# Head of a gated spectral block on one core: the adaptive scale moved into a DFT table, grad_out gated and turned inside the first loop, and the third frequency chunk packed

## The chip, the cores and the metric

The kernel runs on one core of a Trainium2 chip. The metric is device time in microseconds, as the median of repeated executions. The profile is one execution, read as busy times, waits and a chain of releases on the core's engines: PE (TensorE, matrix multiplications), DVE (VectorE), ACT (ScalarE), POOL (GpSimd) and SP (SyncE, here only an issuer of DMAs).

## The reference, cut to what matters

The reference is the forward pass and all gradients of one transformer-like block with 2048 tokens (S) of width 576 (D). With `sa, ca, ga, sb, cb, gb` made from a condition vector `c`:

```python
mod = (silu(c) @ w_mod).reshape(1, 6, 1, 576)      # sa, ca, ga, sb, cb, gb
h = layernorm(x) * (1 + ca) + sa
x = x + ga * irfft2(rfft2(h) * (w_r + 1j * w_i))   # over tokens and width
h = layernorm(x) * (1 + cb) + sb
x = x + gb * (((h @ w_gate) * (h @ w_up)) @ w_down)   # width 4608 inside
# returned: x, and the gradients of x, w_r, w_i, w_gate, w_up, w_down, c, w_mod
```

The gradients need, early on, `grad_out * gb` in two layouts: with tokens on partitions (called `gon` in the kernel) and with width on partitions (`goT`).

## The kernel before, in words

Everything is bf16 with fp32 sums in PSUM. The 2048 tokens are 16 tiles of 128; the width of 576 is four chunks of 128 and one of 64. A Fourier transform is a series of matrix multiplications with tables: `RD` (cosine and sine over the width), `G1` and `BD2` (two steps over the tokens), and `BDA`, `GB`, `IR` for the way back. The 289 frequencies are padded to `FP` = 292, which is 73 groups of 4, taken in 19 chunks (`NCH`) of up to 16 frequencies.

The framework orders instructions itself: each engine has a queue in a fixed order, found at compile time by a list scheduler that follows the program order as priority and simulates durations. `tc.issue_after(x)` puts the instructions of its block behind `x` on `x`'s own queue. At run time an engine works through its queue in order and waits where an input or a buffer isn't ready.

The stages, with the stretches of the profiled execution:

- **Head, 0 to 70 us.** `mod_load`/`mod_make` (L236, L242) multiply the condition by a slice of `w_mod` and leave a row, the same on all partitions, in `modh`. Then `pipeline` runs `s1_norm`, `s1_cols`, `s1_rows` (L284 to L331) over the 16 tiles. `s1_norm` makes the layer norm on ACT (`n1`, L297), multiplies by `1+ca` (L299) and adds `sa` (L301) on DVE, and turns the tile with five PE transposes (L306). `s1_cols` multiplies by `RD` (ten matmuls, L315) and `s1_rows` by `G1` (four, L329 and L330); the result is kept in `VA`. After that loop in program order, `grad_out` is turned tile by tile with six transposes (L347), and two DVE multiplications by a column form of `gb` (`gbT`, read back from `modb_d`) leave `goT` (L348, L349).
- **Chunks, 70 to 134 us.** `s2_turn`, `s2_filter`, `s2_back`, `s2_inv` run over the 19 frequency chunks: transposes, `BD2`, multiplication by the filter, transposes, `BDA`; the planes `A_h` are kept. `u4_groups` put in between them multiply `w_down` by `goT` (L377) and keep the result in DRAM.
- **Way back, 134 to 217 us.** `s3_rows` (six matmuls per tile, L470 and L471), `s3_cols` (twelve, L485) and `s3_norm`, with two `u4_groups` per tile. `s3_norm` loads `x` again in pairs of tiles (`xc`, L495), adds, and makes the second layer norm.
- **Rest of `u4_groups`, 217 to 282 us,** and beside it, on DVE, the multiplication of `gon` by `gb` (L519).
- **Main loop, 282 to about 1280 us,** over 36 blocks of 128 of the inner width: the gated products and their gradients.
- **Tail, about 1280 to 1593 us.** `t1_*`, `t2_*` and `t3_*` are the backward counterparts of the three transform stages; `t3_rows` and `t3_cols` (L1009, L1010, L1022) have the same six and twelve matmuls per tile. The last product with `w_down` (L1113, `u3p`) is put by the scheduler beside them and goes on alone afterwards.

In `s3_rows` and `t3_rows` the 292 frequencies are covered by three windows of 128 that start at `FS = [0, 128, 164]`; the third overlaps the second, and `IR` is zero in the overlap:

```python
for fc in range(3):
    f0 = FS[fc]
    o = upa[:, fc, :] if fc < 2 else upb[:, 0, :]
```

For each window two matmuls of 256 columns follow, one for each plane.

Of the kernel before, what the change touches and what calls it, by code (L numbers as in the profile page):

```python
# [26 lines left out]
EPS = 1e-5  # L27
KD = [128, 128, 128, 128, 64]
RM = [slice(0, 128)] * 4 + [slice(64, 128)]
FS = [0, 128, FP - 128]  # L30
# [5 lines left out]
def _tables():  # L36
# [4 lines left out]
    for m in range(5):  # L41
        d = 128 * m + q
        valid = d < D
# [19 lines left out]
    IR = np.zeros((128, 3, 2, D), f8)  # L63
    d = np.arange(D)
    for fc in range(3):
        ff = FS[fc] + q
        valid = (ff < DF) & (ff >= 128 * fc)
        cf = np.where((ff == 0) | (ff == DF - 1), 1.0, 2.0) / (D * S) * valid
        ang = 2 * np.pi * np.outer(ff, d) / D
        IR[:, fc, 0, :] = np.cos(ang) * cf[:, None]  # L70
        IR[:, fc, 1, :] = -np.sin(ang) * cf[:, None]
# [7 lines left out]

TABS = dict(RD=[128, 5, 2, FP], G1=[128, NT, 3, 128], GB=[128, NT, 3, 128], BD2=[128, 128], BDA=[128, 128], IR=[128, 3, 2, D])  # L80


def build(ctx, tc, A_x, A_w_r, A_w_i, B_w_gate, B_w_up, B_w_down, c_in, w_mod, grad_out,
# [72 lines left out]

    def pipeline(n, steps):
# [26 lines left out]
    gonf = res2.tile([128, NT * D + 64], BF, name="gon")  # L184
    gon = gonf[:, 0:NT * D].rearrange("p (t d) -> p t d", t=NT)

    with ExitStack() as hs:
# [17 lines left out]
        modh = [(u4 if j == MGB else hp1).tile([128, D], BF, name="modh%d" % j) for j in range(6)]  # L205
        VA = hp1.tile([128, NG * 128], BF, name="VA")
        hpp = hp1.tile([128, 3, DP], BF, name="hpp")
        nc.gpsimd.memset(hpp[:, :, D:DP], 0.0)
        nc.gpsimd.memset(gonf[:, NT * D:NT * D + 64], 0.0)
# [13 lines left out]
        nc.vector.tensor_tensor(out=sc_col[:], in0=c_f[:], in1=sig[:], op=MUL)  # L223
        tmp5 = hp1.tile([128, 5], FP32, name="tmp5")
# [4 lines left out]
        sc_bf = hp1.tile([128, 5], BF, name="sc_bf")  # L229
        nc.vector.tensor_copy(sc_bf[:], sc_col[:])  # L230
        nc.vector.tensor_copy(sc_col[:], sc_bf[:])
# [10 lines left out]
        def mod_make(j, wm, eng="v"):  # L242
# [8 lines left out]
            return nc.sync.dma_start(modb_d[:, j, :], modh[j][:]).ins  # L251
# [13 lines left out]
        x_load(0)  # L265
        wms[MSA] = mod_load(MSA)
        T = {"RD": load_table(hp1, "RD", "tA")}
        T["G1"] = load_table(hp1, "G1", "tB")
        mod_make(MCA, wms[MCA])
        first = mod_make(MSA, wms[MSA], "a")  # L270
        with tc.issue_after(first):
            x_load(1)
            wms[MGB] = mod_load(MGB)
            nc.sync.dma_start(gon, go_v)
            x_load(2)
            T["BD2"] = load_table(hp1, "BD2")
            T["BDA"] = load_table(hp1, "BDA")

# [3 lines left out]
        gbT = hp1.tile([128, 5], BF, name="gbT")  # L282

        def s1_norm(t):  # L284
# [6 lines left out]
            if t == 0 or tt == (1 if c4 == 0 else 0):  # L291
                n = 1 if t == 0 else 4 - tt
                nmr = norm_stats(xts[c4][:, tt:tt + n, :], hw2, n, "ln1", rstd1g[:, t:t + n], 4)
                for k in range(n):
                    n1s["nmr", t + k] = nmr[:, k:k + 1]
            n1 = n1s[c4]
            nc.scalar.activation(out=n1[:, tt, :], in_=xts[c4][:, tt, :], func=ACT.Identity, bias=n1s["nmr", t], scale=rstd1g[:, t:t + 1])  # L297
            nm = hw2.tile([128, D], BF, name="nm")
            nc.vector.tensor_tensor(out=nm[:], in0=n1[:, tt, :], in1=modh[MCA][:], op=MUL)  # L299
            hh = hpp[:, t % 3, :]  # L300
            nc.vector.tensor_tensor(out=hh[:, 0:D], in0=nm[:], in1=modh[MSA][:], op=ADD)  # L301
            if tt == 3:
                nc.gpsimd.dma_start(n1_d[:, t - 3:t + 1, :], n1[:])
            pt = fps.tile([128, 5, 128], BF, name="trp", tag="fp")
            for m in range(5):
                nc.tensor.transpose(pt[:, m, :], hh[:, m * 128:(m + 1) * 128], ident[:])  # L306
            hT = hTs[t] = hw2.tile([128, 5, 128], BF, name="hT")
            evac(hT[:], pt[:], eng="a")

        def s1_cols(t):  # L310
            zt = zts[t] = hw2.tile([128, 2, FP], BF, name="zt", bufs=3)
            for cc in range(2):
                zp = fps.tile([128, 512], FP32, name="zp", tag="fp")
                for m in range(5):
                    mm = nc.tensor.matmul(zp[:, :FP], lhsT=hTs[t][:, m, :], rhs=T["RD"][:, m, cc, :], start=(m == 0), stop=(m == 4))  # L315
                evac(zt[:, cc, :], zp[:, :FP], eng="a")
            if t == 1:
                with tc.issue_after(mm.ins):
                    mod_make(MGB, wms[MGB], "a")
                with nc.allow_non_contiguous_dma(reason="tiny column load"):  # L320
                    nc.sync.dma_start(gbT[:, 0:4], modb_d[0, MGB, 0:512].rearrange("(m q) -> q m", q=128))
                    for r in (0, 64):
                        nc.sync.dma_start(gbT[r:r + 64, 4:5], modb_d[0, MGB, 512:576].rearrange("(m q) -> q m", q=64))
# [9 lines left out]
        pipeline(NT, [s1_norm, s1_cols, s1_rows])  # L333
# [8 lines left out]
        goT = u4.tile([128, NT, 5, 128], BF, name="goT")  # L342
        for t in range(NT):
            pt = u4ps.tile([128, 6, 128], BF, name="u4p")
            for m in range(6):
                c0 = t * D + m * 128 if m < 5 else t * D + 448
                nc.tensor.transpose(pt[:, m, :], gonf[:, c0:c0 + 128], ident[:])  # L347
            nc.vector.tensor_tensor(out=goT[:, t, :, :], in0=pt[:, 0:5, :], in1=gbT[:].unsqueeze(2).to_broadcast([128, 5, 128]), op=MUL)  # L348
            nc.vector.tensor_tensor(out=goT[64:128, t, 4, :], in0=pt[64:128, 5, :], in1=gbT[64:128, 4:5].to_broadcast([64, 128]), op=MUL)  # L349
# [39 lines left out]
        A_h = pool("hA", 1).tile([128, 2, NT, FP], BF, name="A_h")  # L389
        with ExitStack() as rc:  # L390
# [16 lines left out]
            def s2_filter(ci):  # L407
                g0, ng, f0, w = dims(ci)
                xp = fps.tile([128, 4, 128], FP32, name="xp", tag="fp")
                for j in range(ng):  # L410
                    nc.tensor.matmul(xp[:, j, :], lhsT=VTs[ci][:, j, :], rhs=T["BD2"][:], start=True, stop=True)
# [21 lines left out]
            def s2_inv(ci):  # L433
# [4 lines left out]
                Ac = A_h[:].rearrange("k c a f -> k (c a) f")[:, :, f0:f0 + w].rearrange("k e (j f) -> k j e f", f=4)  # L438
                evac(Ac, ap_[:, 0:ng, :].rearrange("k j (e f) -> k j e f", f=4), eng="a")
# [23 lines left out]
        def s3_rows(sa):  # L463
            ut = uts[sa] = hw2.tile([128, 3, 256], BF, name="ut", bufs=3)
            upa = fps.tile([128, 2, 256], FP32, name="upa", tag="fp")
            upb = fps.tile([128, 2, 256], FP32, name="upb", tag="fp")
            for fc in range(3):
                f0 = FS[fc]
                o = upa[:, fc, :] if fc < 2 else upb[:, 0, :]
                nc.tensor.matmul(o, lhsT=A_h[:, 0, sa, f0:f0 + 128], rhs=T["GB"][:, sa, 1:3, :].rearrange("k v s -> k (v s)"), start=True, stop=False)  # L470
                nc.tensor.matmul(o, lhsT=A_h[:, 1, sa, f0:f0 + 128], rhs=T["GB"][:, sa, 0:2, :].rearrange("k v s -> k (v s)"), start=False, stop=True)  # L471
            evac(ut[:, 0:2, :], upa[:], eng="a")
            evac(ut[:, 2, :], upb[:, 0, :], eng="v")

        def s3_cols(sa):
# [4 lines left out]
            for h in range(2):  # L480
                yp = fps.tile([128, 512], FP32, name="yp", tag="fp")
                k = 0
                for fc in range(3):
                    for cc in range(2):
                        nc.tensor.matmul(yp[:, 0:288], lhsT=ut[:, fc, cc * 128:(cc + 1) * 128], rhs=T["IR"][:, fc, cc, h * 288:(h + 1) * 288], start=(k == 0), stop=(k == 5))  # L485
                        k += 1
# [222 lines left out]
    with ExitStack() as ts:  # L709
# [108 lines left out]
        with ExitStack() as r1:  # L818
# [44 lines left out]
            def t1_turn(t):  # L863
                pt = ps_fp.tile([128, 5, 128], BF, name="trp", tag="fp")
                for m in range(5):
                    nc.tensor.transpose(pt[:, m, :], rings["gyr"][:, t % 3, wide(m)], ident[:])
# [53 lines left out]
        A_ = pool("rb", 1, "right", stack=rB).tile([128, 2, NT, FP], BF, name="j_A")  # L920
# [20 lines left out]
        with ExitStack() as r2:  # L941
# [35 lines left out]
            def t2_inv(ci):  # L977
# [4 lines left out]
                nc.scalar.copy(A_[:].rearrange("k c a f -> k (c a) f")[:, :, f0:f0 + w].rearrange("k e (j f) -> k j e f", f=4), ap_[:, 0:ng, :].rearrange("k j (e f) -> k j e f", f=4))  # L982
# [19 lines left out]
        def t3_rows(sa):  # L1002
            ut = uts[sa] = c3.tile([128, 3, 256], BF, name="ut", bufs=3)
            upa = ps_fp.tile([128, 2, 256], FP32, name="upa", tag="fp")
            upb = ps_fp.tile([128, 2, 256], FP32, name="upb", tag="fp")
            for fc in range(3):
                f0 = FS[fc]
                o = upa[:, fc, :] if fc < 2 else upb[:, 0, :]
                nc.tensor.matmul(o, lhsT=A_[:, 0, sa, f0:f0 + 128], rhs=T["GB"][:, sa, 1:3, :].rearrange("k v s -> k (v s)"), start=True, stop=False)  # L1009
# [203 lines left out]
```

## Time and profile before

| | us |
|---|---|
| median of 3 runs | 1591.95 (1589.98 to 1597.13) |
| the profiled execution's own time | 1594.8 |
| its span, first to last instruction | 1593.0 |
| PE busy | 1535.0 (96%) |
| DVE busy | 1045.6 (66%) |
| ACT busy | 559.8 (35%) |
| PE busy in 0 to 70 us | 53.4 of 70 |
| PE busy in 70 to 134 us | 64.0 of 64 |
| PE busy in 134 to 217 us | 75.7 of 83 |
| PE busy in 282 to 1280 us | 995.4 of 998 |
| PE busy in 1412 to 1462 us (`t3`) | 47.8 of 50 |
| PE busy in 1462 to 1577 us | 114.6 of 115 |

A matmul's busy time in the profile contains its way through the array, and matmuls overlap; what one costs a full PE is the distance from its start to the start of the next. The mean granted PE clock is 0.992 of full speed.

### The profile page before, as it was taken

The numbers are of one execution on the slowest core, as the hardware profiler recorded it, in microseconds if no ns is written. First come the engines' busy times: TensorE is split into PE (matmuls) and PEld (weight loads), VectorE is DVE, ScalarE is ACT, GpSimd is POOL, SyncE is SP. The second block draws the span as 40 slices with busy tenths as digits, with TensorE's granted clock in tenths as the row PEclk, the third lists the DMA queues.
The fourth block names the chain that finished last, engine by engine and source line by source line (L and its number), as shares of the span: only waits on it lengthen the run. The fifth ranks groups of instructions, "written<-read, shape, count | busy, mean of one in ns | idle before, by whom it ended". The sixth has DMA issues, their size and how long they took to land.

```text
span 1593.0 us, 30039 instructions
## 1 busy us (share of the span) xinstructions
PE 1535.0 (96%) x11370; PEld 1035.0 (65%) x11370; DVE 1045.6 (66%) x2626; ACT 559.8 (35%) x1108; POOL 170.3 (11%) x283
## 2 busy tenths in 40 slices
PE   6999989999999999999999999999999989899997
PEld 4666533567666666766666676666666666677775
DVE  6866763666666666666666666666666774678655
ACT  6666632322222222222222222222222365466022
POOL 0001212101010100101010010101000011100232
PEclk9999999999999999999999999999999999999998
DMA  9869998779877686786868686767857786635775
GB/s 319 275 194 237 242 259 228 166 139 143 141 152 150 130 177 104 158 152 134 162 130 144 140 171 118 164 133 129 180 103 143 191 264 197 218 112 179 286 224 159
DMA packets 485252, 280.64 MB, mean 176 GB/s; under 512 B 407633, under 2 KB 452434, under 8 KB 484210
## 3 DMA queue, kind: packets, MB, share of 16 engines
q1 hardware_dynamic: 459922, 185.65, 55.1%
q0 software_dynamic: 25184, 93.07, 19.8%
q8 instruction: 89, 1.46, 0.4%
q14 instruction: 57, 0.47, 0.1%
HBM read 108.77 MB, written 82.31 MB: 120 GB/s over the span
## 4 chain that ended last, share of the span: by engine, by line
PE 77%; DMA 9%; DVE 7%; issue 3%; ACT 2%; SPq 0%; POOL 0%; DVEq 0%; ACTq 0%; POOLq 0%
PE u57p L572 26%; PE u8p L654 17%; PE gup L625 16%; PE u4p L377 7%; PE gup L620 2%; DMA xc<-in_A_x_dram 2%; DMA n2c<-n_d 2%; DMA Xn<-xn_d 2%; DMA wmj<-in_w_mod_dram 1%; DMA wdB<-in_B_w_down_dram 1%; DVE pr L803 1%; PE u3p L1113 1%; PE yp L485 1%; PE yp L1022 1%; PE zp L315 1%
## 5 line engine op out<-in xcount | busy, mean ns | idle before, releaser
L659 DVE TENSOR_TENSOR acc<-acc,u8p 128x288 f32<-128x288 f32 x1088 | 489.2, 454 | 314.6 <-PE u8p L654 314.2
L654 PE MATMUL u8p<-wT,ggT 128*128 128x288 bf16 x1152 | 327.5, 286 | 2.1 <-DVE acc L659 2.1
L654 PE MATMUL u8p<-wT,guT 128*128 128x288 bf16 x1152 | 327.2, 286 | 0.0
L625 PE MATMUL gup<-h2T,wgu 128*128 128x512 bf16 x1152 | 294.9, 379 | 0.0
L575 ACT CAST so<-u57p 128x288 bf16<-128x288 f32 x216 | 86.0, 398 | 521.4 <-PE u57p L572 515.6
L572 PE MATMUL u57p<-gon,hh_sf 128*128 128x288 bf16 x1152 | 188.6, 286 | 0.4 <-DMA hh_sf<-hhT 0.4
L572 PE MATMUL u57p<-h2p,gg_sf 128*128 128x288 bf16 x1152 | 187.6, 286 | 0.0
L572 PE MATMUL u57p<-h2p,gu_sf 128*128 128x288 bf16 x1152 | 186.2, 286 | 0.0
L625 PEld LDWEIGHTS <-wgu 128*128 128x128 bf16 x1152 | 109.5, 98 | 98.8 <-issue 17.1
L654 PEld LDWEIGHTS <-ggT 128*128 128x128 bf16 x1152 | 112.6, 98 | 67.2 <-issue 14.0
L377 PE MATMUL u4p<-goT,wdT 128*128 128x512 bf16 x656 | 151.1, 379 | 4.4 <-DVE ghh_st L141 3.8
L654 PEld LDWEIGHTS <-guT 128*128 128x128 bf16 x1152 | 112.7, 98 | 56.2 <-issue 2.6
L1113 PEld LDWEIGHTS <-hl 128*128 128x128 bf16 x1152 | 111.5, 98 | 35.7 <-issue 7.5
L572 PEld LDWEIGHTS <-hh_sf 128*128 128x128 bf16 x1152 | 112.6, 98 | 29.0 <-DMA hh_sf<-hhT 0.7
L572 PEld LDWEIGHTS <-gu_sf 128*128 128x128 bf16 x1152 | 112.5, 98 | 28.4
L572 PEld LDWEIGHTS <-gg_sf 128*128 128x128 bf16 x1152 | 112.5, 98 | 28.3
L627 ACT CAST gT<-gup 128x512 bf16<-128x512 f32 x144 | 84.3, 585 | 130.4 <-PE gup L625 130.4
L377 PEld LDWEIGHTS <-wdT 128*128 128x128 bf16 x656 | 61.9, 98 | 77.2 <-issue 11.5
L627 ACT CAST uT<-gup 128x512 bf16<-128x512 f32 x144 | 84.3, 585 | 73.6 <-PE gup L625 73.6
L1113 PE MATMUL u3p<-wdB,hl 128*128 128x288 bf16 x672 | 94.8, 288 | 8.0 <-DMA wdB<-in_B_w_down_dram 7.0
L638 POOL DMA_DIRECT2D hhT_d<-hhT x36 | 33.2, 921 | 504.4 <-DVE hhT L629 475.4
L139 ACT CAST ghh_st<-u4p 128x512 bf16<-128x512 f32 x88 | 51.1, 585 | 68.1 <-PE u4p L377 67.7
(358 smaller groups left out, 1734.0 us busy)
## 6 DMA issues: line engine op xcount, KB each, us to landing
ghhT_d<-ghh_st POOLq DMA_DIRECT2D x36, 512.0 KB, 4.7
ghh<-ghhT_d POOLq DMA_DIRECT2D x36, 512.0 KB, 7.3
hhT_d<-hhT POOLq DMA_DIRECT2D x36, 512.0 KB, 6.6
hl<-hhT_d SPq DMA_DIRECT2D x32, 576.0 KB, 6.9
out_dram<-woT SPq DMA_DIRECT2D x72, 128.0 KB, 2.0
wdn<-in_B_w_down_dram SPq DMA_DIRECT2D x18, 288.0 KB, 4.3
out_dram<-so SPq DMA_DIRECT2D x36, 144.0 KB, 2.6
wgu<-in_B_w_gate_dram SPq DMA_DIRECT2D x18, 256.0 KB, 3.4
```

Of the source, the lines that this page charges most:

```text
L139: nc.scalar.copy(dst, src)
L315: mm = nc.tensor.matmul(zp[:, :FP], lhsT=hTs[t][:, m, :], rhs=T["RD"][:, m, cc, :], start=(m == 0), stop=(m == 4))
L377: nc.tensor.matmul(pt[:], lhsT=wdTs[k][:, j, m, :], rhs=goT[:, 4 * sb4:4 * sb4 + 4, m, :], start=(m == 0 and n == 5), stop=(m == n - 1))
L572: mm = nc.tensor.matmul(pw[0][:, 0:288], lhsT=sf[:, t, :], rhs=rhs_n[:, t, h * 288:(h + 1) * 288], start=(t == 0), stop=(t == NT - 1))
L575: nc.scalar.copy(so[:, h * 288:(h + 1) * 288], pw[0][:, 0:288])
L620: nc.tensor.matmul(pts[-1][:], lhsT=wgu[r, 8, jw * 128:(jw + 1) * 128], rhs=h2T[r, 4 * sb4:4 * sb4 + 4, 4, :], start=True, stop=False)
L625: nc.tensor.matmul(pts[k][:], lhsT=wgu[:, 4 * wi_ + m, jw * 128:(jw + 1) * 128], rhs=h2T[:, ts_, m, :], start=False, stop=(m == 3))
L627: nc.scalar.copy((gT, uT)[wi_][:, ts_, :], pts[k][:])
L638: nc.gpsimd.dma_start(hhT_d[:, :, fb, :].rearrange("tp f x -> f tp x"), hhT[:].rearrange("f (tp ti) p -> f tp (ti p)", ti=2))
L654: nc.tensor.matmul(pu[:, 0:288], lhsT=l_, rhs=r_, start=(k == 0), stop=(k == len(mms) - 1))
L659: nc.vector.tensor_tensor(out=dst, in0=dst, in1=pu[:, 0:288], op=ADD)
L1113: mm = nc.tensor.matmul(p2[:, 0:288], lhsT=hls[fb // 9][:, fb % 9, ti * 128:(ti + 1) * 128], rhs=(wdA[:, fb] if fb < 15 else wdB[:, fb - 1 ...
```

## The change

1. **The scale goes into the table.** `mod_cols` makes `1+ca` as a column (25 matmuls with one column of output); five DVE operations multiply the chunks of `RD` by it, giving `RDm`, and `s1_cols` uses `RDm`. Only the plain layer norm `n1` is turned. Chunks of the width now start at `M0 = [0, 128, 256, 384, 448]`, and the table is zero where the last overlaps, so the zero-padded buffer `hpp` is gone.
2. **The shift goes to frequency zero.** A row added to all tokens only changes the zero token frequency. `shift_rows` computes S times the transform of `sa` once (ten matmuls and a few DVE operations, kept in `zr` as a high and a low part), and each `s2_filter` adds it with one small matmul (`first_k`).
3. **`n1` is made on DVE** with one operation instead of on ACT, and its statistics (`s1_stats`) are made two tiles ahead, in pairs.
4. **`gon` is gated first and turned afterwards**, inside the loop (`go_turn`): one DVE multiplication per tile, five transposes, one plain copy (three of four on ACT). `gon` has 640 columns per tile, and the last 64 are loaded again to fill it. The column `gbT`, its three loads, and the later DVE multiplication of `gon` are gone.
5. **The loop is written out** with lags: norm 0, stats 2 ahead, turn 1, cols 2, rows 4, `go_turn` 6.
6. **Loads.** The `RD` table is loaded ahead of the second slice of `w_mod`; the next loads are queued behind the load of `G1` and no longer behind the store of `sa` (which is gone).
7. **Third chunk packed.** The frequencies from 256 on (33, padded to 64) have their real and imaginary planes side by side in one 128-wide operand (`At`). `rows_back` has four matmuls of 256 columns and two of 128; `cols_back` has five of 288 per half, not six. `keep_planes` fills the planes, with three ACT copies instead of one for the last three chunks. This is used on the way back and in the tail.

```diff
+    def keep_planes(A, At, ps, ng, f0, w):
+        if f0 < FM:
...
+        for pl, c in ((0, 1), (1, 0), (2, 1)):
...
+    def rows_back(A, At, sa, ps_a, ps_b, GB):
+        for fc in range(2):
+            for c in range(2):
+                nc.tensor.matmul(ps_a[:, fc, :], lhsT=A[:, c, sa, 128 * fc:128 * fc + 128], rhs=GB[:, sa, 1 - c:3 - c, :].rearrange("k v s -> k (v s)"), start=(c == 0), stop=(c == 1))
+        for k in range(2):
+            nc.tensor.matmul(ps_b, lhsT=At[:, sa, 1 - k:3 - k, :].rearrange("k c f -> k (c f)"), rhs=GB[:, sa, 1 + k, :], start=(k == 0), stop=(k == 1))
+    def cols_back(ut, yp, IR, h):
+        for k in range(5):
+            nc.tensor.matmul(yp[:, 0:288], lhsT=ut[:, 128 * k:128 * k + 128], rhs=IR[:, k, 0, h * 288:(h + 1) * 288], start=(k == 0), stop=(k == 4))
...
+        def mod_cols(j, wm):
+            ps = fps.tile([128, 512], FP32, name="modcol", tag="fp")
+            for d in range(5):
+                for m in range(5):
+                    nc.tensor.matmul(ps[:, d:d + 1], lhsT=wm[:, m, M0[d]:M0[d] + 128], rhs=sc_bf[:, m:m + 1], start=(m == 0), stop=(m == 4))
...
+        T = {"RD": load_table(hp1, "RD", "tA")}
         wms[MSA] = mod_load(MSA)
-        T = {"RD": load_table(hp1, "RD", "tA")}
         T["G1"] = load_table(hp1, "G1", "tB")
-        mod_make(MCA, wms[MCA])
-        first = mod_make(MSA, wms[MSA], "a")
+        nc.vector.tensor_copy(opc[:], mod_cols(MCA, wms[MCA])[:])
+        for m in range(5):
+            nc.vector.tensor_scalar(out=RDm[:, m].rearrange("q c f -> q (c f)"), in0=T["RD"][:, m].rearrange("q c f -> q (c f)"), scalar1=opc[:, m:m + 1], scalar2=None, op0=MUL)
+        first = tab_ins["G1"]
         with tc.issue_after(first):
             x_load(1)
             wms[MGB] = mod_load(MGB)
             nc.sync.dma_start(gon, go_v)
+            nc.sync.dma_start(gonw[:, :, D:DP], go_v[:, :, 512:D])
             x_load(2)
...
+        def shift_rows():
+            col = mod_cols(MSA, wms[MSA])
+            s_rep = hw2.tile([128, 5, 128], BF, name="s_rep", tag="hT")
+            his = hw2.tile([128, 2, FP], BF, name="zhi", tag="zt", bufs=3)
...
-            nc.scalar.activation(out=n1[:, tt, :], in_=xts[c4][:, tt, :], func=ACT.Identity, bias=n1s["nmr", t], scale=rstd1g[:, t:t + 1])
-            nc.vector.tensor_tensor(out=nm[:], in0=n1[:, tt, :], in1=modh[MCA][:], op=MUL)
-            nc.vector.tensor_tensor(out=hh[:, 0:D], in0=nm[:], in1=modh[MSA][:], op=ADD)
+            nc.vector.tensor_scalar(out=n1[:, tt, :], in0=xts[c4][:, tt, :], scalar1=rstd1g[:, t:t + 1], scalar2=n1s["nmr", t], op0=MUL, op1=ADD)
...
+        def go_turn(t):
+            nc.vector.tensor_tensor(out=gonw[:, t, :], in0=gonw[:, t, :], in1=modh[MGB][:], op=MUL)
+            pt = u4ps.tile([128, 5, 128], BF, name="u4p")
+            for m in range(5):
+                nc.tensor.transpose(pt[:, m, :], gonw[:, t, m * 128:(m + 1) * 128], ident[:])
+            evac(goT[:, t, :, :], pt[:], eng="v" if t % 4 == 3 else "a")
+        s1_stats(0)
+        s1_stats(1)
+        for k in range(NT + 6):
+            for s_, lag in ((s1_norm, 0), (s1_stats, -2), (s1_turn, 1), (s1_rows, 4), (go_turn, 6), (s1_cols, 2)):
+                if 0 <= k - lag < NT:
+                    s_(k - lag)
...
-        for t in range(NT):
-            pt = u4ps.tile([128, 6, 128], BF, name="u4p")
-            for m in range(6):
-                nc.tensor.transpose(pt[:, m, :], gonf[:, c0:c0 + 128], ident[:])
-            nc.vector.tensor_tensor(out=goT[:, t, :, :], in0=pt[:, 0:5, :], in1=gbT[:].unsqueeze(2).to_broadcast([128, 5, 128]), op=MUL)
-            nc.vector.tensor_tensor(out=goT[64:128, t, 4, :], in0=pt[64:128, 5, :], in1=gbT[64:128, 4:5].to_broadcast([64, 128]), op=MUL)
...
+                nc.tensor.matmul(xp[:, 0:ng, :].rearrange("k j (c a f) -> k j c a f", c=2, a=NT)[:, :, :, 0, :], lhsT=first_k[:], rhs=zr[:, g0:g0 + ng, :, :], start=False, stop=True)
...
-        with tc.issue_after(h2_made[-1]):
-            for t in range(NT):
-                nc.vector.tensor_tensor(out=gon[:, t, :], in0=gon[:, t, :], in1=modh[MGB][:], op=MUL)
```

More of the change, by code (lines that the diff above doesn't have):

```diff
@@ L62, in _tables @@
                 BDA[q0, c0] = cs_; BDA[q1, c0] = -sn_; BDA[q0, c1] = sn_; BDA[q1, c1] = cs_
-    IR = np.zeros((128, 3, 2, D), f8)
+    IR = np.zeros((128, 5, 1, D), f8)
     d = np.arange(D)
[L65 to L71, printed above, removed]
+    for pl in range(5):
+        for half in range(2):
+            cc = pl % 2 if pl < 4 else half
+            f0 = 128 * (pl // 2) + 64 * half if pl < 4 else FM
+            ff = f0 + np.arange(64)
+            valid = ff < DF
+            cf = np.where((ff == 0) | (ff == DF - 1), 1.0, 2.0) / (D * S) * valid
+            ang = 2 * np.pi * np.outer(ff, d) / D
+            IR[64 * half:64 * half + 64, pl, 0, :] = (np.cos(ang) if cc == 0 else -np.sin(ang)) * cf[:, None]
     import ml_dtypes
@@ L183, in build @@
     h2n = h2p[:, :, 0:D]
-    gonf = res2.tile([128, NT * D + 64], BF, name="gon")
-    gon = gonf[:, 0:NT * D].rearrange("p (t d) -> p t d", t=NT)
+    gonw = res2.tile([128, NT, DP], BF, name="gon")
+    gon = gonw[:, :, 0:D]
     with ExitStack() as hs:
@@ L204, in build @@
         hw2 = pool("hc1", 2, "right", stack=r1)
-        modh = [(u4 if j == MGB else hp1).tile([128, D], BF, name="modh%d" % j) for j in range(6)]
+        RDm = hw2.tile([128, 5, 2, FP], BF, name="RDm", bufs=1)
+        modh = {j: (u4 if j == MGB else hp1).tile([128, DP if j == MGB else D], BF, name="modh%d" % j) for j in range(6) if j not in (MSA, MCA)}
+        zr = hp1.tile([128, NG, 2, 4], BF, name="zr")
+        first_k = hp1.tile([128, 128], BF, name="first_k")
+        nc.gpsimd.memset(first_k[:], 0.0)
+        for r in (0, 64):
+            nc.gpsimd.memset(first_k[r:r + 1, 0:1], 1.0)
         VA = hp1.tile([128, NG * 128], BF, name="VA")
-        hpp = hp1.tile([128, 3, DP], BF, name="hpp")
-        nc.gpsimd.memset(hpp[:, :, D:DP], 0.0)
-        nc.gpsimd.memset(gonf[:, NT * D:NT * D + 64], 0.0)
         wdn2 = u4.tile([128, 2, 2, DP], BF, name="wdn2")
@@ L250, in mod_make @@
                     evac(modh[j][:, h * 288:(h + 1) * 288], ps[:, 0:288], eng=eng)
-            return nc.sync.dma_start(modb_d[:, j, :], modh[j][:]).ins
+                if j == MGB and h == 1:
+                    nc.vector.tensor_copy(modh[j][:, D:DP], ps[:, 224:288])
+            nc.sync.dma_start(modb_d[:, j, :], modh[j][:, 0:D])
+        def mod_cols(j, wm):
[3 more added lines that the diff above has]
+                    nc.tensor.matmul(ps[:, d:d + 1], lhsT=wm[:, m, M0[d]:M0[d] + 128], rhs=sc_bf[:, m:m + 1], start=(m == 0), stop=(m == 4))
+            col = hp1.tile([128, 5], BF, name="modc%d" % j)
+            nc.vector.tensor_scalar(out=col[:], in0=ps[:, 0:5], scalar1=1.0 if j == MCA else 0.0, scalar2=None, op0=ADD)
+            return col
         xts = []
@@ L281, in build, with s1_stats @@
         hTs, zts, n1s = {}, {}, {}
-        gbT = hp1.tile([128, 5], BF, name="gbT")
+        def shift_rows():
+            col = mod_cols(MSA, wms[MSA])
+            s_rep = hw2.tile([128, 5, 128], BF, name="s_rep", tag="hT")
+            his = hw2.tile([128, 2, FP], BF, name="zhi", tag="zt", bufs=3)
+            nc.vector.tensor_copy(s_rep[:], col[:].unsqueeze(2).to_broadcast([128, 5, 128]))
+            for cc in range(2):
+                zs = fps.tile([128, 512], FP32, name="zs", tag="fp")
+                for m in range(5):
+                    nc.tensor.matmul(zs[:, 0:FP], lhsT=s_rep[:, m, :], rhs=T["RD"][:, m, cc, :], start=(m == 0), stop=(m == 4))
+                hi = his[:, cc, :]
+                nc.vector.tensor_scalar(out=hi, in0=zs[:, 0:FP], scalar1=float(S), scalar2=None, op0=MUL)
+                nc.vector.tensor_copy(zr[0:64, :, cc, :], his[0:64, cc, :].rearrange("p (g f) -> p g f", f=4))
+                nc.vector.scalar_tensor_tensor(out=zr[64:128, :, cc, :], in0=zs[64:128, 0:FP].rearrange("p (g f) -> p g f", f=4), scalar=float(S), in1=his[64:128, cc, :].rearrange("p (g f) -> p g f", f=4), op0=MUL, op1=SUB)
+        grp = {}
+        def s1_stats(t):
+            g0 = t if t < 2 else t - t % 2
+            if t == g0:
+                grp[g0] = [hw2.tile([128, 2] + sh, FP32, name="ln1_" + nm) for nm, sh in (("st", [2, nc.vector.BN_STATS_DIM]), ("mv", [nc.vector.BN_AGGR_DIM]), ("nmr", []))]
+            st, mv, nmr = grp[g0]
+            xt = xts[t // 4][:, t % 4, :]
+            for h in range(2):
+                nc.vector.bn_stats(out=st[:, t - g0, h, :], in_=xt[:, h * 288:(h + 1) * 288])
+            nc.vector.bn_aggr(out=mv[:, t - g0, :], in_=st[:, t - g0, :, :])
+            if t < 2 or t % 2:
+                n, rs = t + 1 - g0, rstd1g[:, g0:t + 1]
+                nc.scalar.activation(out=rs, in_=mv[:, 0:n, 1], func=ACT.Sqrt, bias=eps_t[:], scale=1.0)
+                nc.vector.reciprocal(out=rs, in_=rs)
+                nc.vector.scalar_tensor_tensor(out=nmr[:, 0:n], in0=mv[:, 0:n, 0], scalar=-1.0, in1=rs, op0=MUL, op1=MUL)
+                for k in range(n):
+                    n1s["nmr", g0 + k] = nmr[:, k:k + 1]
         def s1_norm(t):
@@ L318, in s1_cols @@
                 with tc.issue_after(mm.ins):
+                    shift_rows()
                     mod_make(MGB, wms[MGB], "a")
[L320 to L323, printed above, removed]
         def s1_rows(t):
@@ L388, in build @@
         r1.close()
-        A_h = pool("hA", 1).tile([128, 2, NT, FP], BF, name="A_h")
+        A_h = planes(pool("hA", 1), "A_h")
         with ExitStack() as rc:
@@ L463, in s3_rows @@
         def s3_rows(sa):
-            ut = uts[sa] = hw2.tile([128, 3, 256], BF, name="ut", bufs=3)
+            ut = uts[sa] = hw2.tile([128, 640], BF, name="ut", bufs=3)
             upa = fps.tile([128, 2, 256], FP32, name="upa", tag="fp")
[L466 to L473, printed above, removed]
+            upb = fps.tile([128, 512], FP32, name="upb", tag="fp")
+            rows_back(*A_h, sa, upa, upb[:, 0:128], T["GB"])
+            evac(ut[:, 0:512], upa[:].rearrange("f c s -> f (c s)"), eng="a")
+            evac(ut[:, 512:640], upb[:, 0:128], eng="v")
         def s3_cols(sa):
@@ L481, in s3_cols @@
                 yp = fps.tile([128, 512], FP32, name="yp", tag="fp")
[L482 to L486, printed above, removed]
+                cols_back(ut, yp, T["IR"], h)
                 evac(yb[:, sa % 2, h * 288:(h + 1) * 288], yp[:, 0:288], eng="a")
@@ L919, in build @@
         rB = ExitStack()
-        A_ = pool("rb", 1, "right", stack=rB).tile([128, 2, NT, FP], BF, name="j_A")
+        A_ = planes(pool("rb", 1, "right", stack=rB), "j_A")
         gYs = {}
@@ L1002, in t3_rows @@
         def t3_rows(sa):
-            ut = uts[sa] = c3.tile([128, 3, 256], BF, name="ut", bufs=3)
+            ut = uts[sa] = c3.tile([128, 640], BF, name="ut", bufs=3)
             upa = ps_fp.tile([128, 2, 256], FP32, name="upa", tag="fp")
[L1005 to L1009, printed above, removed]
-                nc.tensor.matmul(o, lhsT=A_[:, 1, sa, f0:f0 + 128], rhs=T["GB"][:, sa, 0:2, :].rearrange("k v s -> k (v s)"), start=False, stop=True)
-            nc.scalar.copy(ut[:, 0:2, :], upa[:])
-            nc.scalar.copy(ut[:, 2, :], upb[:, 0, :])
+            upb = ps_fp.tile([128, 512], FP32, name="upb", tag="fp")
+            rows_back(*A_, sa, upa, upb[:, 0:128], T["GB"])
+            nc.scalar.copy(ut[:, 0:512], upa[:].rearrange("f c s -> f (c s)"))
+            nc.scalar.copy(ut[:, 512:640], upb[:, 0:128])
         def t3_cols(sa):
```

70 lines of the change are left out of this document (39 added, 31 removed).

## The prediction

> **What bounds the kernel now.** I read the slices first, then busy time by stage, the chain of waits, the head's costliest groups, and the waits on the way back.
>
> ```profile
> PE   6999989999999999999999999999999989899997
> DVE  6866763666666666666666666666666774678655
> DMA  9869998779877686786868686767857786635775
> ```
> A slice is 40 us. PE is full but for the first and a few late ones.
>
> ```profile
> 0.00:70.00 70.00, 53.41 (x456) 38.08 (x457) 54.61 (x159) 48.80 (x99) 4.25 (x15) 0.95 0.89 298
> 70.00:134.00 64.00, 64.00 (x513) 38.61 (x512) 43.01 (x119) 39.16 (x75) 5.85 (x11) 1.00 0.70 209
> 134.00:217.00 83.00, 75.67 (x477) 45.82 (x475) 53.55 (x163) 53.74 (x108) 18.14 (x34) 1.00 1.04 252
> 1412.00:1462.00 50.00, 47.81 (x416) 36.59 (x417) 38.86 (x100) 34.29 (x76) 1.61 (x3) 1.00 0.58 176
> 1462.00:1577.00 115.00, 114.58 (x920) 90.72 (x918) 74.42 (x187) 25.78 (x50) 30.54 (x51) 1.00 0.74 233
> ```
> The columns are length, then PE, PEld, DVE, ACT and POOL busy, PE clock, DMA share and GB/s. PE idles in the head (16.6 us) and on the way back (7.3 us, with DMA at 1.04); elsewhere near the change it is full. So time comes from filling the head, and from taking matmuls out where PE is full.
>
> ```profile
> 60.45 1.34 PE zp L315 x10
> 62.09 0.82 DVE goT L348
> 62.92 0.41 DVE VA L141
> 63.67 1.57 DVE goT L348 x2
> 65.26 0.50 DVE goT L349 x2
> 65.79 1.57 DVE goT L348 x2
> 67.38 0.50 DVE goT L349 x2
> 67.91 1.57 DVE goT L348 x2
> 69.85 5.57 PE u4p L377 x25
> ```
> The head ends with 8 us in which DVE finishes `goT` and PE waits; from 69.85 us on PE is full. Ahead of that it has done 12 transposes, 8 `xp` and 6 `u4p` of later stages: 12x0.057 + 8x0.057 + 6x0.216 = 2.4 us at their distances from start to start. So PE is full as from 67.4 us.
>
> ```profile
> L297 ACT ACTIVATE n<-xt,ln_nmr,rstd1g 128x576 bf16<-128x576 bf16 x16 | 14.0, 881 | 0.2 <-DVE ln_nmr L154 0.2
> L348 DVE TENSOR_TENSOR goT<-u4p,gbT 128x640 bf16<-128x640 bf16 x16 | 12.8, 819 | 1.6 <-PE u4p L347 1.3
> L301 DVE TENSOR_TENSOR hpp<-nm,modh 128x576 bf16<-128x576 bf16 x16 | 7.3, 454 | 0.5
> L299 DVE TENSOR_TENSOR nm<-n,modh 128x576 bf16<-128x576 bf16 x16 | 7.2, 452 | 2.6 <-ACT n L297 2.4
> L349 DVE TENSOR_TENSOR goT<-u4p,gbT 64x128 bf16<-64x128 bf16 x16 | 4.5, 294 | 0.4
> ```
> Four DVE groups of the change take 31.8 us of the head's 54.6.
>
> ```profile
> DVE x L501 <- DMA xc<-in_A_x_dram: 13.0, 5, 4.0
> SPq L362 <- DMA wdT<-wdn: 29.9, 6, 8.8
> ```
> On the way back DVE waits 13.0 us for the loads `xc`, which stand on SP behind loads that wait for the transposes `wdT`. DVE's copy of `ut`, which PE needs, is queued behind that.
>
> **The head, part by part.** Per tile, DVE loses L299, L301, L348, L349 (0.45+0.45+0.82+0.29 = 2.02 us) and gains `n1`, the gating over 640 columns and a quarter of the copies. No row has DVE's one-input operation with two scalars in bf16; I take 0.45 us, the multiplication's row (bounds 0.3 and 0.53, the latter L812 from fp32). Gating is 0.45x640/576 = 0.50; a quarter of a copy about 0.2. With statistics (2x0.41+0.2), VA (0.46) and the statistics' small operations (0.17), DVE goes from 3.5 to 2.8 us a tile. ACT loses 0.88 and gains 0.75x0.69: 2.8 to 2.5. PE needs 14 matmuls of 292 columns at 0.122 and ten transposes at 0.057: 2.3 us. Before, the zp groups start 2.98 us apart on average (15.64 to 60.38 over 15 tiles) and 2.53 at the end. I take 2.7.
>
> By the Trainium skill (VectorE: DVE Perf Modes, the perf-mode tier table) a bf16 `tensor_scalar` in SBUF runs at four elements a cycle and `tensor_tensor` at two; `n1` would then be near 0.3 us and DVE 2.65 a tile, an estimate from that page that the sum does not use.
>
> Start: the first zp stood at 15.64, behind the row of `sa`. Now it needs 25 one-column matmuls from about 6.5 us (0.057 each warm as the transposes, twice that cold: 1.4 to 2.9), two small DVE operations (0.4) and five of 584 columns (0.45 each, 2.3): 12.0, bounds 11 and 14. `RD` is issued one load of 720 KB earlier. Inserted behind it are the row of `1+ca`, `shift_rows`, its 25 columns and one more row: some 20 matmuls at 0.122 and 25 at 0.057, 3.9 us. The last zp comes at 12 + 15x2.7 + 3.9 = 56.4; its group takes 1.3, and the last four `go_turn` about 0.8 each (ACT's copy 0.69 on top of DVE), so PE is full from 60.9. **Gain 6.4 us**; bounds 57.4 (pace 2.53, start 11) and 67.1 (pace 2.98, start 14): 10.0 and 0.3.
>
> Loads: `x`, `gb`, `gon` are issued some 7 us sooner, but DMA is already 0.97 busy from 10 to 60 us, so they land little sooner. New is the load of 2048 pieces of 128 bytes. Bounds: by bytes, 256 KB at 298 GB/s, 0.9 us; by pieces, 14297 hardware-queue packets took 72% of 16 engines for 70 us, 56 ns each, so 7.2 us. I take 3, mostly paid back by three `gbT` loads (640 pieces of two bytes) and the store of `sa`. It stands ahead of `x`'s third load on SP, and the first gating on DVE waits for it, with `n1` and VA behind. In the sum it is nothing, since the order puts gating six tiles late; uncovered it costs up to 7.
>
> **Chunks.** 19 small matmuls at 0.03 to 0.057 on a full PE, 1.0. The last chunk has three ACT copies, not one, ahead of `upb` (L139's 128-column form, 0.265): 0 to 0.53, I take 0.4, and again in the tail. **Loss 1.4 here, 0.4 there.**
>
> **Way back.** Per tile `yp` goes from 12 to 10 matmuls (2x0.1225) and `up` from six at 0.109 to four and two of 0.057 (0.10): 0.35 us, 5.6 for 16 tiles. Bounds 0 (loads pace it) and 5.6; DMA is full, but PE idles only 7.3 of 83 us: **3.0**. The 16 multiplications of `gon` removed from DVE (16x0.37 = 5.9 us, 216 to 224) hide under `u4p`: PE is idle 0.1 us after 217. Gain 0.
>
> **Tail.** `t3` saves the same 5.6 us of PE, which is 96% busy there; what is freed must be filled with `u3p`, and `u3p` alone keeps PE full up to 1577. Bounds 0 and 5.6: **4.5**. The main loop is untouched: `gon` only has a wider row.
>
> **Sum:** 6.4 - 1.4 + 3.0 + 4.5 - 0.4 = 12.1 us. The profiled execution's own time is 1594.8 (span 1593.0), 2.85 above the median; 12.1 less is 1582.7, or 1579.9 against the median of 1591.95.
>
> **Rivals.**
> 1. *Loads pace the head.* For: DMA 0.97 busy, 128-byte pieces ahead of the third part of `x`; a zt buffer used for the row of `1+ca` is free only after its store, queued behind all those loads. Against: before, DVE waited for `xt` 2.1 us in all. The head then gains 0.3: 1579.9 + 6.1 = 1586.0. By the Trainium skill (DMA: Bandwidth & Descriptors, Specifications) pieces under 512 bytes fall below line rate; counted as 512 bytes each, the load is 1 MB and takes 3.5 us, an estimate with that page. No row here shows a load of 2048 such pieces.
> 2. *What PE saves turns into waits* on the way back and in `t3`. For: DMA 1.04, the `xc` waits; in `t3` PE already waits for ACT in each tile. Then 7.5 is lost: 1587.4.
> 3. *Slower: `xc` falls one `wdT` turn later on SP.* The order is made anew, and PE asks for `w_down` 8% sooner of a full DMA. If four of the eight `xc` wait 8.8 us (the longest wait for `wdT`) where they now wait about 3, DVE and then PE lose 4x5.6 = 22: 1579.9 + 22 = 1602. It decides once DVE's wait for `xc` exceeds 13 + 20 = 33 us. Against: PE queues two `u4` groups a tile, whose cover has so far held PE's loss at 7.3.
>
> **How the numbers follow.** The measurement can tell some 0.5%, 8 us, from no change. My forecast (gain 9 to 18) 0.52; rival 1 alone 0.12 and rival 2 alone 0.14, both near the line of 1584; both together or a part of rival 3, 0.10; rival 3 in full 0.12. Faster: 0.52 and four tenths of rivals 1 and 2, 0.62. Slower, 0.12. Same, 0.26. Low end: all upper bounds, 10.0 - 0.6 + 5.6 + 5.6 = 20.6, 1571. High end: 1596, past both rivals of lost gains; outside are rival 3 and a little on the low side.
>
> **What would show it.** Right: PE full from about 61 us; zp 2.7 us apart, first at 12; chunks 1 us longer; `yp` x10; the way back 3 us shorter; `u3p` ending 12 us earlier. Wrong: DVE waiting for `gonw` or a zt buffer in the head; `xc` waits over 33 us; PE idle growing in `t3`.

## The result, and the profile after

The change made the kernel slower: 1602.71 us (median of 16 runs, 1592.63 to 1607.3) against 1592.72 for the kernel before beside it; the ratio is 1.0053, 95% interval 1.0038 to 1.0069. The forecast was 1579.9. The profiled execution took 1604.12 us (span 1602.3), 9.3 more than the one of before.

The slices of after (40 us each) show the loss late:

```profile
PE   6999899999999999999999999999999968999897
DVE  7565643666666666666666666666665754678665
DMA  9988996867686776867676786847774877444785
```

PE's 33rd slice, 1282 to 1322 us at the tail's entry, reads 6, where it read 8 before. The first three stages in after, and two rows of that entry (1280 to 1340 and 1340 to 1366 us):

```profile
0.00:70.00 70.00, 55.35 (x523) 41.21 (x524) 46.78 (x164) 45.13 (x99) 6.08 (x18) 1.00 0.99 300
70.00:134.00 64.00, 62.62 (x522) 38.26 (x520) 39.18 (x112) 40.36 (x86) 5.70 (x11) 1.00 0.86 218
134.00:217.00 83.00, 75.18 (x462) 42.38 (x461) 53.03 (x165) 53.28 (x107) 18.58 (x35) 1.00 1.06 263
1280.00:1340.00 60.00, 40.62 (x320) 29.39 (x319) 30.50 (x79) 22.83 (x44) 8.28 (x18) 0.83 0.77 239
1340.00:1366.00 26.00, 25.69 (x223) 18.08 (x222) 12.48 (x28) 16.55 (x38) 2.19 (x4) 1.00 0.49 181
```

The two rows of the entry in before:

```profile
1280.00:1340.00 60.00, 52.19 (x489) 39.56 (x487) 39.90 (x102) 37.25 (x75) 9.17 (x17) 0.97 0.74 220
1340.00:1366.00 26.00, 17.60 (x153) 12.26 (x153) 10.12 (x28) 10.15 (x22) 3.65 (x10) 0.93 1.01 349
```

In 1280 to 1366 us PE is busy 66.3 us; before it was 69.8 (52.2 + 17.6). That difference is small, but what PE does there is not the same, as the fences under the experiments show.

The chain through the end of the head:

```profile
47.04 14.45 DMA wdT<-wdn
61.48 0.05 issue
61.53 4.49 PE u4p L460 x20
...
73.00 10.62 DMA ghhT_d<-ghh_st
```

PE is full from 61.5 us, and what released it there is the transposes `wdT` (a wait of 2.1 us), not `goT` on DVE as before. The DVE groups that answer to the four of before:

```profile
L413 DVE TENSOR_TENSOR gon<-gon,modh 128x640 bf16<-128x640 bf16 x16 | 7.1, 477 | 0.0
L374 DVE TENSOR_SCALAR n<-xt,rstd1g,ln_nmr 128x576 bf16<-128x576 bf16 x16 | 6.5, 415 | 0.1
L144 DVE COPY goT<-u4p 128x640 bf16<-128x640 bf16 x4 | 1.9, 472 | 0.4 <-PE u4p L416 0.4
L318 DVE TENSOR_SCALAR RDm<-T_RD,opc 128x584 bf16<-128x584 bf16 x5 | 1.5, 368 | 0.3 <-DMA T_RD<-tab_RD 0.3
```

They take 17.0 us where the four took 31.8. On the way back DVE waits for `xc` about as long as before (13.0):

```profile
DVE x L576 <- DMA xc<-in_A_x_dram: 11.9, 4, 4.1
```

So the 9.3 us come from elsewhere. I read the first and last start of some PE groups, which split the span. In us:

| kernel | first `upa` | first `gup` | last `u8p` | last `u3p` | span |
|---|---|---|---|---|---|
| before | 133.8 | 282.6 | 1268.6 | 1577.8 | 1593.0 |
| after | 130.6 | 274.3 | 1265.0 | 1587.9 | 1602.3 |

The first `gup` (start of the main loop) comes 8.3 us earlier. From there to the last `u8p` it is 990.7 us, 4.7 longer. From there to the last `u3p` it is 322.9, 13.7 longer; the rest is 0.8 shorter. -8.3 + 4.7 + 13.7 - 0.8 = 9.3. Two places to explain: the tail's entry, and the main loop's start.

**The tail's entry.** Waits there (1256 to 1372 us) in after; the two on `out_dram<-woT` have no counterpart before:

```profile
DVE jk L924 <- DMA n2c<-n_d: 14.7, 2, 9.5
PE csA L841 <- DMA n2c<-n_d: 12.0, 3, 9.9
DVE b_Vp L144 <- DMA out_dram<-woT: 4.0, 1, 4.0
ACT b_Vp L142 <- DMA out_dram<-woT: 1.0, 1, 1.0
```

`b_Vp` is the tail's buffer for the result of `t1_rows`; `woT` is a ring of three buffers of the main loop, from which the last weight gradients are stored. They have nothing to do with each other, unless they share memory. By the program's allocation they do: before, the third `woT` buffer ends at byte 129504 of a partition and `b_Vp` starts at 132448. After, `gon` is 1920 bytes wider, which moves all main loop buffers up (`woT` ends at 131424), and the tail's inverse table is smaller (5760 bytes against 6912, in a place shared with `RD`'s 5840, so that the place now takes 5856, a multiple of 32, and no longer 6912), which moves `b_Vp` down by 1056 to 131392. The last 32 bytes of one are the first of the other.

### The profile page after: what moved, and what is told of

Read it like the earlier page. It is cut to its first block, busy times and chain, and to the rows that moved or that the text cites. A ratio compares the mean times of both kernels' runs of the same rounds, so it can differ in the third digit from the quotient of the medians.

```text
span 1602.3 us, 30033 instructions
## 1 busy us (share of the span) xinstructions
PE 1531.0 (96%) x11359; PEld 1029.4 (64%) x11359; DVE 1025.4 (64%) x2606; ACT 553.9 (35%) x1118; POOL 173.0 (11%) x286
## 4 chain that ended last, share of the span: by engine, by line
PE 80%; DMA 9%; DVE 4%; issue 4%; ACT 2%; SPq 1%; POOL 0%; ACTq 0%; DVEq 0%; POOLq 0%
PE u57p L644 26%; PE u8p L726 17%; PE gup L697 15%; PE u3p L1177 7%; PE u4p L460 6%; PE gup L692 2%; DMA wdT<-wdn 2%; DMA xc<-in_A_x_dram 1%; PE zp L958 1%; DMA n2c<-n_d 1%; DMA wdn<-in_B_w_down_dram 1%; DMA woT<-so 1%; DMA hh_sf<-hhT 1%; DMA ghhT_d<-ghh_st 1%; DMA hl<-hhT_d 1%
## 5 line engine op out<-in xcount | busy, mean ns | idle before, releaser
L144 DVE CAST ghh_st<-u4p 128x512 bf16<-128x512 f32 x56 | 38.6, 690 | 64.3 <-PE u4p L460 55.6
```

What stands on the lines that cost most here:

```text
L144: nc.vector.tensor_copy(dst, src)
```

## The experiments

Times are medians of the kernel and ratios to the kernel before on the same chip.

### Take the 32 bytes away

```diff
+        pool("gap", 1).tile([128, 32], BF, name="gap")
         Vp = pool("vp", 1).tile([128, NG, 128], BF, name="b_Vp")
```

> The changed kernel with one unused tile of 64 bytes per partition put ahead of the tail's b_Vp, so that b_Vp starts 32 bytes above the end of the main loop's third woT buffer instead of 32 bytes below it; nothing else differs. Theory A (the shared 32 bytes make the tail's first transform wait for the last woT stores, and the recording puts t1's steps behind the u57 products for it): t1's steps lie among the u57 products again, the 13 to 14 us lost between 1270 and 1372 us come back, and the time is 1584 to 1590 us (1602.7 - 13.5 = 1589.2, and up to 4.1 less by the tail's shorter way back). Rival B (the earlier transfers of the main loop, or the stall on hh_sf at 294 us, make n2c and hl late at the tail's entry): 1600 to 1605 as after. Rival C (the packed third chunk is itself slow in the tail): 1600 to 1605 as after.

Measured: 1585.59 us, ratio 0.9962 (0.9943 to 0.998). An unused tile of 64 bytes turned a slower kernel into one faster than before. Theory A held, B and C fell.

### Give the kernel before the same 32 bytes, and nearly so

```diff
+            bpool("gap", 1).tile([128, 976], BF, name="gap")     # 944 in the second kernel
             wot = bpool("wot", 3)
...
-        sel = tl.tile([128, 2, 128], FP32, name="sel")
+        sel = tl3.tile([128, 2, 128], FP32, name="sel")
```

> The kernel before, with nothing of the change in it, its buffers moved alone: an unused tile of 1952 bytes ahead of the woT buffers, and the tail's tile sel (1024 bytes) allocated behind b_Vp instead of ahead of it, so that b_Vp and the third woT buffer share 32 bytes. Theory A: the before kernel then shows the same loss: 1592.7 + 13 to 14 = 1604 to 1608 us, with a wait of b_Vp on the woT stores, and last u3p some 13 us later. Rivals B and C: 1592 to 1594, since neither transfers nor arithmetic have changed.

> As the run before it (before with buffers moved), but the unused tile is 64 bytes shorter: b_Vp starts 32 bytes above the end of the third woT buffer. Theory A: 1592 to 1594 us, as before, with no wait of b_Vp on a store. Were the moved tiles or another overlap the cause of a loss in the run before it, it would be lost here too (1604 to 1608).

Measured: with the shared 32 bytes 1603.49 us, ratio 1.0074 (1.005 to 1.0099); with the tile 64 bytes shorter 1594.06, ratio 1.0015 (0.9995 to 1.0035). The kernel before shows a loss of the same kind with nothing of the change in it: 11.8 us by its ratio, a little under the 13 to 14 expected. The evacuations into `b_Vp` on DVE, in the order before with shared bytes, before without, after, after with the gap (count, then shortest, median and longest in ns, then first and last start in us):

```profile
L141 DVE CAST b_Vp<-vp x16: 451/460/463, 1313.7 to 1366.8; 128x292 bf16<-128x292 f32 x16
```
```profile
L141 DVE CAST b_Vp<-vp x16: 447/460/463, 1276.4 to 1352.8; 128x292 bf16<-128x292 f32 x16
```
```profile
L144 DVE CAST b_Vp<-vp x16: 453/462/463, 1315.8 to 1370.5; 128x292 bf16<-128x292 f32 x16
```
```profile
L144 DVE CAST b_Vp<-vp x16: 453/461/463, 1265.2 to 1340.1; 128x292 bf16<-128x292 f32 x16
```

With shared bytes the first tile goes into `b_Vp` 37 and 51 us later (7 of the 51 were there at the last `u8p`); in after that is just behind the stores of `woT` that were issued at 1313.5 and 1313.9 us. The wait seen at run time is only 5.0 us. The larger part is the order: the compile-time scheduler knows of the dependency, so on PE 14 of the 16 tiles of `t1_cols` stand behind the last `u57p` of the main loop (in after at 1314.3 us), where in the two programs without shared bytes 12 of the 16 stand ahead of it. In the two fences below, with one row each for 1256 to 1280, 1280 to 1320, 1320 to 1345 and 1345 to 1372 us, the first number behind the length is PE's time on `zp` (the matmuls of `t1_cols`); PE clock, DMA share and GB/s follow. After:

```profile
1256.00:1280.00 24.00, 3.31 (x20) 0.99 0.80 210
1280.00:1320.00 40.00, 2.07 (x15) 0.83 0.66 193
1320.00:1345.00 25.00, 7.03 (x39) 0.86 0.99 335
1345.00:1372.00 27.00, 12.97 (x88) 1.00 0.34 127
```

After with the gap:

```profile
1256.00:1280.00 24.00, 7.22 (x50) 1.00 0.55 131
1280.00:1320.00 40.00, 8.72 (x50) 0.91 0.65 212
1320.00:1345.00 25.00, 8.62 (x60) 1.00 0.80 242
1345.00:1372.00 27.00, 0.00 (x0) 0.87 0.69 257
```

In after the independent matmuls `u57p` are spent by 1314 us while the transform of 14 tiles is still to come, each step waiting for the one before; it ends at 1369 us (last `zp`) instead of 1339. Where PE loses the time can be read: in 1255 to 1372 us it waits 18.8 us for loads in after (`n2c` 12.0, `hl` 6.8) and 20.5 in before with shared bytes, against 12.7 in the gap kernel and 15.0 in before, and its granted clock falls further (0.83 over 60 us in both kernels with shared bytes, 0.94 in the gap kernel, 0.97 in before). What the wait on the stores and what the order cost was not tried apart.

### The parts alone

The change's head with the tail's chunks as before, and the tail's packed chunk in the kernel before. In both `b_Vp` is clear of `woT`: each half of the change moves one of the two, and only both together make them meet.

> The changed kernel with the third chunk of the tail (t2, t3) as in before; the head keeps the whole change. The tail's inverse table is then 6912 bytes again and b_Vp lies 1024 bytes clear of woT. Theory A: t1 among the u57 products; the first gup at 274 us (8.3 earlier than before); by the prediction's terms 6.4 - 1.4 + 3.0 = 8.0 is kept, 1584.7; if the stall on hh_sf and the lower clock at 294 to 320 us stay, 3.7 is kept, 1589.0. Rival B (early transfers of the main loop make the tail's entry late): 1600 to 1605. Rival C: 1585 to 1589 here too, but then the run with the 64-byte tile stays at 1602.

> The kernel before with the packed third chunk in the tail alone (t2's keep_planes, t3's rows and columns, a packed inverse table beside the old one, which the head keeps); b_Vp is 1888 bytes clear of woT. The prediction's tail term is 4.5 - 0.4 = 4.1: 1587 to 1588 us. The head alone against the kernel with the 64-byte tile gave 4.7. If the savings turn into waits on loads of u3p: 1590 to 1592.

Measured: the head alone 1590.29, ratio 0.9993 (0.9972 to 1.0014); the tail alone 1588.13, ratio 0.9964 (0.9944 to 0.9983). Neither shows the loss of 13 us, as theory A says. The tail's term is there, but the head is worth about nothing in the timed runs, where 8.0 was expected or 3.7 with the stall left.

### The main loop's start

In after, in the gap kernel and in the head alone, the first `u57p` of the main loop waits. The row of after, and the row of before:

```profile
PE u57p L644 <- DMA hh_sf<-hhT: 3.1, 1, 3.1
```
```profile
PE u57p L572 <- DMA hh_sf<-hhT: 0.4, 1, 0.4
```

SP's queue there in after (start, duration of the issue), and below it the issue of `hh_sf` in before:

```profile
283.55 2.02 SPq L715 DMA_TRANSPOSE gu_sf<-guT  x1
285.67 7.07 SPq L715 DMA_TRANSPOSE hh_sf<-hhT  x1
292.83 3.93 SPq L715 DMA_TRANSPOSE gg_sf<-ggT  x1
```
```profile
293.81 5.57 SPq L643 DMA_TRANSPOSE hh_sf<-hhT  x1
```

Before, `hh_sf` was issued at 293.81 and its first use stood at 302.9, 9.1 us later; here it takes 11.6. The issues stand 11.2 and 11.4 us behind the first `gup`. The wait costs more than its length where the clock falls with it: in 290 to 310 us PE's granted clock is 0.83 in after, 0.91 in the gap kernel and 1.00 in the head alone, after waits of 3.1, 3.0 and 3.2 us, and the stretch from the first `gup` to the last `u8p` is 4.7, 4.2 and 1.6 us longer than before's 986.0. The Trainium skill (TensorE: Matmul & The Clock Gate, HAM oscillation) names PE gaps of over about 3.4 us as what brings the low clock. Here it came behind gaps just below that in two profiles of three, and not behind the longest of them. I put `hh_sf` and `gg_sf` ahead of `gu_sf`, in the gap kernel, in before and in the head alone, and tested the addresses by moving before's main loop buffers to where after has them:

```diff
-  with tc.high_priority(...):
+  with tc.high_priority(...), (tc.issue_after(turned.ins) if fb == 0 and sfs[fb] else ExitStack()):
       turned = nc.sync.dma_start_transpose(out=sf[:], ...)
```

> The changed kernel with the 64-byte tile, and in the main loop's first turn hh_sf and gg_sf issued ahead of gu_sf (which is not used until two blocks later). In the profiles of the changed kernel, of the one with the 64-byte tile and of the head alone, PE waits 3.0 to 3.2 us for hh_sf some 23 us into the main loop and runs at a granted clock of 0.8 to 0.9 after it; in before and its moved copies it waits 0 to 0.4. Theory D (the head's gain is partly given back at that wait): hh_sf is issued 2 us earlier and lands 2 us earlier, the wait falls to 1 us or below, and 2 to 4 us come back: 1581.5 to 1583.5 us. Rival E (the wait is a gap that later transfers would have made anyway, further on in the loop): the wait goes, and the time stays at 1584.5 to 1587.

> The kernel before with an unused tile of 1920 bytes ahead of all buffers of the main loop: they lie where the changed kernel's wider gon puts them (hh_sf at the same address as there), and b_Vp is still 1024 bytes clear of woT. Were the 3 us wait on hh_sf a matter of addresses: PE waits about 3 us on hh_sf here too and the time is 1595 to 1597 us. Were it a matter of the head's earlier end (what is still in flight then): no such wait, and 1591 to 1594. Theory A for the tail: t1 stays among the u57 products in both cases, so nowhere near 1604.

> The kernel before with the main loop's first hh_sf and gg_sf issued ahead of the first gu_sf, nothing else. In before PE waits 0.4 us for hh_sf, so theory D (the order helps only where the wait is) expects 0 to 0.5 us: the ratio to before within 0.2% of 1. If the order is worth the same 3 to 4 us here, then it is a gain of its own, and the head's loss at that place is not shown by it.

> The head alone (tail's third chunk as in before, b_Vp 1024 bytes clear of woT), with hh_sf and gg_sf issued ahead of gu_sf. The head alone gave 0.9993 with a 3.2 us wait on hh_sf. Theory D with the prediction's terms for the head (6.4 - 1.4 + 3.0 = 8.0) expects 0.9950, some 8 us under before; by the measured steps (the first gup 8.7 us earlier on the mean of the profiles, nothing given back at hh_sf) 8 to 9. If half of the head's gain is lost further on, at the tail's entry: 0.9970 to 0.9980.

Measured: gap kernel with the new order 1582.03, ratio 0.9939 (0.9916 to 0.9962), the fastest of all; before moved 1591.78, ratio 0.9986 (0.9968 to 1.0004), with no wait at that place; before with the new order 1591.14, ratio 1.0 (0.9982 to 1.0017); head with it 1588.19, ratio 0.9973 (0.9953 to 0.9993). So the order seems to be worth 3 to 4 us where the wait stood (0.9962 to 0.9939 and 0.9993 to 0.9973). The timed runs alone do not show it, since the intervals of each pair overlap; the traces do show the wait gone in both and the stretch to the last `u8p` shorter (990.2 to 984.7 us, 987.6 to 985.2). In before the order is worth nothing in the timed runs, and addresses are not the wait's cause. The head with the new order was expected at 0.9950; it came out at what had been named for half of the head's gain lost further on, though its profile shows no loss at the tail's entry (313.3 us from the last `u8p` to the last `u3p`, 311.7 in before with the new order). SP's queue in the fastest kernel:

```profile
280.67 2.32 SPq L715 DMA_TRANSPOSE hh_sf<-hhT  x1
283.09 6.52 SPq L715 DMA_TRANSPOSE gg_sf<-ggT  x1
289.67 3.10 SPq L715 DMA_TRANSPOSE gu_sf<-guT  x1
```

The long issue stays with the second transpose, which is now `gg_sf`, and PE's wait is gone. Why the second takes 7 us with the new head and 5.2 to 5.9 with the old one is open: the other transfers at that place (`hhT_d`, `ghh`) are issued at the same distance from the first `gup` in both. One lead that was not tried: in after, the gap kernel and the head alone a packet of the instruction queue (q14) moves at 287, 281 and 281 us, inside that long issue, and in none of the kernels with the old head does one.

## Why the prediction was wrong, step by step

Eleven profiles, six with the old head and five with the new one, give each step with less noise than one pair does. They are means, and some spread: the way back takes 142.0 to 149.3 us with the old head, and the row clear of `woT` 309.2 to 315.6 with the old chunk (before itself has 309.2). The two rows with shared bytes are one profile each.

| us | old head | new head | gained | predicted |
|---|---|---|---|---|
| first `upa` (head and chunks) | 134.0 | 128.7 | 5.3 | 6.4 - 1.4 = 5.0 |
| first `upa` to first `gup` (way back) | 145.0 | 141.3 | 3.7 | 3.0 |
| first `gup` | 279.0 | 270.0 | 9.0 | 8.0 |
| first `gup` to last `u8p`, orders as in before or after | 985.8 | 989.5 | -3.7 | 0 |
| the same, `hh_sf` first | 984.4 | 985.0 | | |
| last `u8p` to last `u3p`, clear of `woT`: old chunk, packed chunk | 312.7 | 309.4 | 3.3 | 4.1 |
| the same with the shared bytes: old chunk, packed chunk | 322.9 | 322.9 | 0 | |

In the last two rows the columns are the tail's old and packed chunk, whatever the head.

- **Head: right in its times, in part by luck.** First zp at 13.4 us (12.0 forecast, within 11 to 14), the last at 56.9 (56.4), PE full from 61.5 (60.9). But the 3.2 us that the sum puts behind the last zp for four `go_turn` are not what was spent there: the last of their transposes starts at 59.1, and then PE waits 2.1 us for `wdT`, which the sum does not have. In the gap kernel and the head alone `wdT` is there in time, PE waits 0.2 us for `goT` and is full from 60.7 and 59.8. DVE's 3.5 us a tile before add up to 3.7 by the terms given; the pace of 2.7 did not rest on it. The price of `n1` was too high: two of them in a row start 0.35 us apart, the five operations on `RD` 0.28, where I took 0.45. By the Trainium skill (VectorE: DVE Perf Modes, the perf-mode tier table) this form runs at four elements a cycle; the estimate of 0.3 us from that page lies between the two.
- **The load of 2048 short pieces** kept SP 8.96 us in issuing it, where I had bounded its price by 0.9 and 7.2. No engine waited for it: the lag of six tiles covered it, as the sum assumed. For `x`, whose third load stands behind it, DVE waited 1.6 us in all, 2.1 before.
- **Way back, tail: right in mechanism; chunks: not measured apart from the head** (5.3 us for both, 5.0 forecast). PE takes the savings; rival 2 fell (PE waits 2.0 us for `ut` in `t3`, 1.4 before). In `t3` the packed chunk alone gave a ratio of 0.9964, 5.7 us.
- **Rival 3 fell**: DVE's wait for `xc` was 11.9 us, far from 33. The slower outcome that I gave 0.12 came about by another mechanism.
- **The failed step is one sentence: "The main loop is untouched: `gon` only has a wider row."** The wider row moved every buffer behind it. Together with the smaller table that put `b_Vp` on `woT` and cost 13.5 us with the packed chunk (322.9 - 309.4); as ratios, 1.0053 against 0.9962, 14.5 us. With the old chunk it is 10.2 (322.9 - 312.7), or 9.4 by the ratios (1.0074 against 1.0015). The tail's gain was lost in it whole: with shared bytes both chunks take 322.9. Nothing in the profile of before showed the 2944 bytes between the two; the sum held prices of instructions and none for memory.
- **Also in that sentence:** that the main loop is untouched. It lost some 3.7 us on the wait for `hh_sf`, in the profiles as in the ratios (0.9962 to 0.9939). The wider row is not the cause here, since before with its buffers moved has no such wait.

Put right, the account reads 12.1 forecast, 14.5 lost to shared bytes, 3.7 to `hh_sf`: a loss of 6.1, where 8.4 was measured (0.53%). The rest is that the gains themselves fell short: without both losses the kernel gains 0.61%, 9.7 us (6.1 to 13.4). The parts add up: 0.27% for the head with the new order and 0.36% for the tail. What stays open is the head's size in timed runs, 4.3 us (1.1 to 7.5) where the profiles show 9. Its runs spread from 1579.66 to 1595.88 us, and the profiled execution of the head alone is near the low end of its own (1585.23 against a median of 1590.29). This is so for most of the table: the profiled executions lie 2.4 us below the medians of their kernels on average with the new head, and 1.2 above with the old one. These 3.6 us are the larger part of the 4.7 between 9.0 and 4.3, so the table's gains are on the high side, and the timed 4.3, about half of the 8.0 forecast, is the better figure for the head. After, the gap kernel and the one with the new order are the same program up to the main loop, and their first `gup` stands at 274.3, 267.8 and 270.6, with the differences in chunks and way back, where the chain runs through `wdT` and `ghhT_d`. No longer execution of the head alone was profiled, so in which stage those lose is not shown.

## What to carry to other kernels

When a tile changes size, list what lies at its old and new end in every later stage: a dependency on shared memory reaches the compile-time order, and 32 bytes cost more here than the whole arithmetic gained. In the trace it shows as a buffer that waits for a transfer of a stage it has nothing to do with; an unused tile of a few bytes tests it. A gain early in a long kernel is to be followed to the end by the starts of a few groups, stage by stage, since each boundary can take some of it back.

## What the runs showed of the hardware

- SP was held 8.96 us by issuing one DMA of 256 KB in pieces of 128 bytes, and 6.79 by the next ordinary one; a 2.3 MB load ahead of them took 0.63 us to issue.
- Of three transposes of 512 KB issued one behind the other beside plain copies, the second held SP longest (5.2 to 7.2 us against 1.8 to 2.3 for the first), whichever tile it moved.
- The granted clock went with PE's idling: 0.83 in 1280 to 1340 us of after, where PE was busy 40.6 of 60 us, 0.94 in the gap kernel with 50.8, and 0.97 in before with 52.2. In 290 to 310 us it fell behind single waits of 3.1 and 3.0 us, and not behind one of 3.2.
